# A top-k attention with two MLPs on one core: the planner's numbers set anew, two batches' value norms put at mid-run, heads and weight chunks scaled by VectorE

## The chip, the cores and the metric

The kernel runs on one core of a Trainium2 chip. The metric is the device time of one execution in microseconds (us), inputs and output in the chip's memory. The five engines are named as in the profile: PE (TensorE, with PEld for its weight loads), DVE (VectorE), ACT (ScalarE), POOL (GpSimd) and SP (SyncE, which here only issues DMAs).

## The reference

```python
scores = scale * q @ k.T                        # 4 batches, 8 heads, 576 x 64
kth = the 32nd largest of each row
attn = softmax(where(scores >= kth, scores, -1e9))
x = (attn @ v), heads side by side               # 2304 tokens x 512
h = x @ w_in                                     # 512 x 2048
g = where(h >= 1, h, where(h <= -1, 0, (h + 1)**2 / 4))
y = g @ w_out                                    # 2048 x 512
h2 = maximum(y @ w2_in, 0)
out = (h2 * h2) @ w2_out
```

All inputs and the output are float32. The result is to be close to float32, so that each operand is scaled by a power of two and split in a high and a low half in float16; a product is then three float16 matmuls.

## The kernel before

Tokens go in 18 tiles T of 128; tiles 4 and 13 hold the end of one batch and the start of the next, 64 rows each. A tile and a head make a slot, 144 in all. In a slot PE makes the scores (`s`, four matmuls, eight in tiles 4 and 13), DVE finds the 32 largest of each row with four MAX8 and three MATCH_REPLACE8, POOL makes a bias `nb`, ACT makes mask, exponential and the high half `pc`, POOL the low half, SP turns `pc` by a DMA (`pT`), and PE multiplies with the values (14 matmuls, called attend). After four heads `x_part` takes the reciprocal sums (`rs`) and scales the heads from PSUM to `x`.

The MLPs run behind, one group (a quarter of a tile's hidden layer in one of the two MLPs) to a slot, from slot 12 on: 12 matmuls of 512 columns into `h` and 12 into `o`. The first `tr` tiles of each MLP make `h` already transposed, with 48 matmuls of 128 columns; for later tiles SP turns the activations (`g<-gr`).

The weights `i1`, `o1`, `i2`, `o2` come in 16 chunks each. `w_decode` packs a chunk (POOL, ACT, DVE), `w_norm` adds its squares on PE (`gram`), `w_scale` makes the scale and `w_split` scales and splits, in the way that a letter in `w_i1` to `w_o2` says: `p` has ACT write the high half and PE form the low half (a float32 matmul and a float16 one into `lo`), which ACT copies out; `a`, `g` and `q` scale in place on ACT, POOL or DVE, then ACT writes the high half and POOL subtracts for the low one; `Q` does the same as `q`. Keys and values are scaled and split likewise by `k_prep` and `v_prep`, on POOL and ACT, or on ACT and DVE for the chunks in `dk` and `dv`. Their scales come from `norm` (ACT squares with a sum) and `kv_scale` (a short chain on DVE and PE). `meet_consts`, `mlp1_consts` and `mlp2_consts` make small per-batch constants on DVE from the value scales.

Nothing is issued as it is written. Every operation is noted with a key, its step (8 steps to a slot, `at(u, ...)`), and `Book.order` simulates five in-order engines with estimated costs and takes, on each engine, the ready operation with the lowest key. So PLAN's steps and margins set the order on each engine, and the waits follow from the data. Its `slack` delays what PE takes up after another engine, past a given time; `warm` fills planned idle time of PE with dummy matmuls (`gram<-ones`). `gshift` delays MLP groups by steps.

Of the kernel before, what the change touches and what calls it, by code (L numbers as in the profile page):

```python
# [13 lines left out]
ALU = mybir.AluOpType  # L14
# [18 lines left out]


PLAN = dict(
    slack=(260, 0.5, 0.5),
    dps={'i1': 16, 'o1': 16, 'i2': 16, 'o2': 14},
    warm=(15, 300, 0.6),
    soon={'s': 8, 'att': 8, 'a': 8, 'x': 24},
    kch=(0, 0, 0, 1), vch=(0, 0, 1), scale=(0, 1, 2, 3, 4, 5), dch=(0, 1, 3), qch=(0, 0, 3, 4), k0=(-5, -4, -2),  # L40
    ka=(0, 1), qa=(0,), d0=(-8, -6, -4, -2), l0=(-9, -6), n0=(0, 1, 0, 1, 2, 3), q01=-5, v0l=0, v0k=1, lag=1, tbufs=(1, 1), v0n=(5, 7, 9, 11), v0s=14, vn=112, vnd=6,
    vnl=18, vs=276, meet=283, mc1=287, m2c0=121, m2c1=300, v0=(21, 25, 29, 33, 37, 41, 45, 49), kv1=(254, 10, 289, 6),
    kv2=(525, 17, 553, 14), kv3=(828, 10, 862, 7), knl=69, knd=4, knll=4, ksl=34, ql=58, qs=50,
    qsch=(2, 7, 8, 9, 9, 10, 28), qp0=21, qp1=6,
    dec_i1=(8, 10, 12, 14, 16, 18, 20, 22, 24, 26, 28, 30, 32, 34, 36, 38),
    dec_o1=(43, 45, 47, 49, 51, 53, 55, 57, 59, 61, 63, 65, 67, 69, 71, 73),
    dec_i2=(76, 78, 80, 82, 84, 86, 88, 90, 92, 94, 96, 98, 100, 102, 104, 106),
    dec_o2=(109, 111, 113, 115, 117, 119, 121, 123, 126, 128, 130, 136, 138, 146), li1=4, ldl=5,
    half=((15, 150, 158), (14, 161, 168)), wn=1, ws_i1=45, ws_o1=80, ws_i2=113, ws_o2=183, sp_i1=55, sp_o1=87,
    sp_i2=120, sp_o2=190, spch=(0, 0, 1), spd_i1=8, spd_o1=8, spd_i2=8, spd_o2=8, mc0=55, N0=12, early=0,  # L50
    gshift=(0, 0, 0, 0, 0, 0, 0, 0, 0, 0, 0, 3, 3, 3, 3, 1), xu=4, xch=(0, 1, 2, 4, 4, 5),
    ych=(0, 1, 2, 3, 5, 6, 10, 10, 73), yu=36, ou=28, z0=200, g_in=(9, 9, 9, 9), g_out=(20, 22, 23, 26), g_act=11,
    g_gate=13, g_split=15, scores=-6, below=8, wbufs=4, md=(), exp=9, bias=7, phi=10, plo=11, ptr=13, att=30, acopy=29, li1d=3, lo1=0, lo1d=0, xu0=2,
    dk=(0, 1, 2), dv=(8, 11, 5, 7), dq=(), odd=0, klead=10, vlead=5, sbufs=3,
    vbufs=8,
    w_i1="pppppppppppppppp", w_o1="pgpgpgpgpgpgpgpg", w_i2="agagagagagagagag", w_o2="agagagagagagagag",
    phd=(), ghd=(), sq=(), u0=-6,
    prio=(3, 0, 0, 2, 2, 3, 4, 5, 5, 1, 7), gbufs=(2, 2), tr=(3, 3), p_tr=18, p_out=8, p_end=4,
)


# [89 lines left out]
class Book:  # L151
# [37 lines left out]
    def note(self, engine, method, fn, args, kwargs):  # L189
# [57 lines left out]
        deps.discard(op.n)  # L247
        op.deps = deps
        op.banks = {v.tile for v in views if v.tile.ring.psum}
        if engine == "POOL" or engine == "DVE" and sum(not v.tile.ring.psum for v in ins if v.elements() > 64) > 1:  # L250
            op.banks.add("port")
        if method == "dma_start_transpose":
            op.banks.add("turn")
# [36 lines left out]
    def order(self):  # L290
# [36 lines left out]
        while len(out) < len(ops):  # L327
            best = None
            for e in engines:
                if now[e]:  # L330
                    t = free[e]
                elif soon[e]:
                    t = max(free[e], soon[e][0][0])
                else:
                    continue
                if best is None or t < best[0]:
                    best = (t, e)
            if best is None:
                raise RuntimeError("no order: " + "; ".join(f"{r.kwargs['tag']}: {len(r.waiting)}" for r in self.rings.values() if r.waiting))
            t, e = best  # L340
            while soon[e] and soon[e][0][0] <= t:
                op = ops[heapq.heappop(soon[e])[1]]
                heapq.heappush(now[e], (op.key, op.n))
            op = ops[heapq.heappop(now[e])[1]]
            if not taken.isdisjoint(op.opens):
                shut.append(op)
                free[e] = t
                continue
            later = apart(op, t)
            if later > t:  # L350
# [12 lines left out]
            if op.load:
                wire = max(wire, t + 1.6) + took
                end = wire + 0.7
            elif op.move == "dma_start_transpose":
                wire = max(wire, t + 1.1) + took
                end = wire + 0.4
            else:
                end = t + took  # L370
            for b in op.banks:
                held.setdefault(b, {})[e] = end + 0.08
            out.append(op)
            for n in op.succ:
                s = ops[n]
                gap = 0.03 if s.engine == e else 0.08 if s.engine != "PE" or end < PLAN["slack"][0] else PLAN["slack"][1]
                s.ready = max(s.ready, end + gap if s.engine != "PE" or e != "PE" else t)
                s.missing -= 1
                if not s.missing:
                    ask(s)  # L380
            for r in op.tiles:
                r.left -= 1
                r.end = max(r.end, end + 0.08)
                if not r.left:
                    ring = r.ring
                    while ring.waiting and not ring.given[-ring.bufs].left:
                        ask(ops[heapq.heappop(ring.waiting)[1]])
# [32 lines left out]
def tile_topk_attention_mlp_mlp(  # L420
# [269 lines left out]
    def kv_scale(name, b):  # L690
        s, i = kvs[name]
        n2 = kvn2[name][:, b, 0:NNORM] if b == 0 else kvn2[name][:, b]
        return global_scale(s[:, b : b + 1], i[:, b : b + 1], n2, f"{name}{b}")

# [70 lines left out]
    def v_prep(b, h):  # L767
        on_dve = 8 * b + h in PLAN["dv"]

        def scale():  # L770
            t = ld["v", b, h]
            if not on_dve:
                POOL.tensor_scalar(t, t, sv[:, b : b + 1], 1.0, op0=ALU.mult, op1=ALU.mult)
            vs = pool.tile([P, 2, 5, D1], F16, tag="vst", name=f"vst_{b}_{h}", bufs=PLAN["vbufs"])
            POOL.memset(vs[:, 0, :, D : D + 1], 1.0)
            POOL.memset(vs[:, 1, :, D : D + 1], 0.0)
            vst[b, h] = vs

        def split_hi():
            ACT.activation(vst[b, h][:, 0, :, 0:D], ld["v", b, h].rearrange("p (c d) -> p c d", d=D), AF.Copy, **(dict(scale=sv[:, b : b + 1]) if on_dve else {}))  # L780

        def split_lo():
            vs = vst[b, h]
            t3 = ld.pop(("v", b, h)).rearrange("p (c d) -> p c d", d=D)
            if on_dve:
                DVE.scalar_tensor_tensor(
                    vs[:, 1, :, 0:D], t3, sv[:, b : b + 1], vs[:, 0, :, 0:D], op0=ALU.mult, op1=ALU.subtract
                )
            else:
                POOL.tensor_tensor(vs[:, 1, :, 0:D], t3, vs[:, 0, :, 0:D], op=ALU.subtract)  # L790
# [227 lines left out]
    def x_part(T, half):  # L1018
# [18 lines left out]
        def scale():  # L1037
# [3 lines left out]
            if T in (4, 13):  # L1041
                to = x[64 * half : 64 * half + 64].rearrange("p (j b a) d -> p a b j d", a=2, b=2)
                for b in range(2):
                    for a in range(2):
# [33 lines left out]

    def mlp1_consts(c0, c1):
# [244 lines left out]
        at(PLAN["v0n"][i], norm, 0, i, "v")  # L1324
    chain(PLAN["v0s"], SCALE, kv_scale, "v", 0)
    for i in range(6 * NNORM):
        at(PLAN["vn"] + PLAN["vnd"] * i - PLAN["vnl"], norm_load, v, 1 + i // (2 * NNORM), i % (2 * NNORM), "v")
        at(PLAN["vn"] + PLAN["vnd"] * i, norm, 1 + i // (2 * NNORM), i % (2 * NNORM), "v")
    for b in range(1, B):
        chain(PLAN["vs"] - 12 + 6 * (b - 1), SCALE, kv_scale, "v", b)  # L1330
    chain(PLAN["meet"], range(4), meet_consts)
    chain(PLAN["mc1"], range(11), mlp1_consts, 1, 6)
    chain(PLAN["m2c0"], range(3), mlp2_consts, 0, 1)
    chain(PLAN["m2c1"], range(3), mlp2_consts, 1, 6)
    for h in range(8):
        v_chain(0, h, PLAN["v0"][h])
    for b in (1, 2, 3):
# [153 lines left out]
```

## Time and profile before

| | us |
|---|---|
| median of three runs | 1086.64 (1085.31 to 1087.84) |
| the profiled execution | 1082.34 |
| its span, first to last instruction | 1080.5 |

The profile is of one execution, 1.84 us of which lie around the span. It counts an engine as busy while an instruction of it runs; the chain of waits goes back from the last instruction, at each step to what released it. All operations are recorded through one helper, so that every row has line 407, and the rows are told apart by tile names.

### The profile page before, as it was taken

To read this page: it belongs to the slowest core of one execution; us is meant where nothing else is said; L and a number is where in the kernel's file an instruction comes from. 1 tells how busy PE (TensorE), PEld (TensorE's weight loads), DVE (VectorE), ACT (ScalarE), POOL (GpSimd) and SP (SyncE) were. 2 spreads that over 40 slices of the span, in tenths; PEclk is the share of its full clock that TensorE was granted. 3 is DMA by queue.
4 is the path that set the end of the run, shared out by engine and by line. 5 is a ranking of instruction groups with operands and counts; after the bars stand their busy time and mean duration, and the time that the engine had idled before them with its cause. 6 is when DMAs were issued, how large, how long until landed. Compare 5 with 4: busy or idle time off the path is not lost.

```text
span 1080.5 us, 23997 instructions
## 1 busy us (share of the span) xinstructions
PE 1009.5 (93%) x8426; PEld 555.3 (51%) x8426; DVE 901.9 (83%) x1992; ACT 866.0 (80%) x1605; POOL 673.5 (62%) x1056
## 2 busy tenths in 40 slices
PE   3977789889999999999999999999999999999997
PEld 2853467666555654544444545444444444544443
DVE  4999886988899999999999999999899999991100
ACT  4679998999878788877988897988688888875442
POOL 3595878879776665657785665667674646553221
PEclk9999999999999999999999999999999999999999
DMA  8999876764667486889977677788776675664333
GB/s 222 309 339 230 234 217 161 128 145 89 137 123 136 82 135 125 169 132 165 178 138 141 117 134 135 158 150 171 135 144 135 115 134 106 125 111 90 69 66 62
DMA packets 438057, 159.14 MB, mean 147 GB/s; under 512 B 416432, under 2 KB 423600, under 8 KB 437936
## 3 DMA queue, kind: packets, MB, share of 16 engines
q1 hardware_dynamic: 434512, 156.76, 70.9%
q10 hardware_dynamic: 3424, 0.85, 0.5%
q8 instruction: 66, 1.08, 0.4%
q14 instruction: 55, 0.45, 0.1%
HBM read 55.31 MB, written 4.72 MB: 56 GB/s over the span
## 4 chain that ended last, share of the span: by engine, by line
PE 66%; ACT 9%; DMA 8%; POOL 7%; DVE 5%; issue 4%; SPq 1%; POOLq 0%; DVEq 0%; ACTq 0%
PE h L407 28%; PE o L407 27%; PE s L407 9%; DMA pT<-pc 3%; POOL wall L407 3%; ACT wall L407 2%; DVE m L407 2%; ACT W L407 2%; DVE W L407 1%; POOL pc L407 1%; PE gram_i L407 1%; ACT r L407 1%; ACT pc L407 1%; DVE wall L407 1%; PE lo_i L407 1%
## 5 line engine op out<-in xcount | busy, mean ns | idle before, releaser
L407 PE MATMUL o<-wall,g 128*128 128x512 f16 x1728 | 434.4, 380 | 7.6 <-POOL g L407 2.1
L407 DVE MAX8 m<-W 128x8 f32<-128x576 f32 x432 | 325.0, 756 | 6.7
L407 PEld LDWEIGHTS <-g 128*128 128x128 f16 x1728 | 160.7, 98 | 192.3 <-issue 11.4
L407 POOL TENSOR_TENSOR pc<-W,pc 128x64 f16<-128x64 f32 (+1 forms) x288 | 205.8, 736 | 66.7 <-ACT pc L407 62.0
L407 POOL TENSOR_TENSOR gr<-r,gr 128x512 f16<-128x512 f32 x120 | 139.3, 1161 | 163.3 <-ACT gr L407 148.8
L407 DVE MATCH_REPLACE8 W<-m,W 128x576 f32<-128x576 f32 x288 | 213.8, 743 | 0.0
L407 PE MATMUL h<-wall,T_x 128*128 128x512 f16 x720 | 168.5, 379 | 0.0
L407 PE MATMUL h<-wall,T_y 128*128 128x512 f16 x720 | 168.0, 379 | 0.0
L407 ACT ACTIVATE W<-W,nb,esc 128x576 f32<-128x576 f32 x144 | 124.4, 864 | 14.5 <-POOL nb L407 9.1
L407 ACT ACTIVATE W<-s,m 128x576 f32<-128x576 f32 x144 | 105.9, 736 | 30.0 <-DVE m L407 21.1
L407 DVE MAX8 m<-s 128x8 f32<-128x576 f32 x144 | 109.2, 759 | 22.1 <-PE s L407 17.4
L407 PEld LDWEIGHTS <-T_y 128*128 128x128 f16 x720 | 69.4, 98 | 81.1
L407 PEld LDWEIGHTS <-pT 128*128 128x128 f16 (+1 forms) x2240 | 82.7, 100 | 54.5 <-issue 15.0
L407 PEld LDWEIGHTS <-wall 128*128 128x128 f16 (+1 forms) x1408 | 85.7, 100 | 48.3 <-DVE wall L407 23.5
L407 PEld LDWEIGHTS <-T_x 128*128 128x128 f16 x720 | 69.0, 98 | 80.0 <-issue 0.4
L407 DVE MATCH_REPLACE8 W<-m,s 128x576 f32<-128x576 f32 x144 | 107.6, 748 | 0.0
L407 PE MATMUL s<-kst,qT 128*128 128x64 f16 (+3 forms) x640 | 98.2, 290 | 9.8 <-ACT W L407 7.8
L407 POOL TENSOR_SCALAR nb<-m,esc 128x1 f32<-128x1 f32 x144 | 53.4, 371 | 85.5 <-DVE m L407 67.9
L407 PE MATMUL s<-vst,pT 128*128 128x65 f16 (+1 forms) x2240 | 90.2, 194 | 15.3 <-DMA pT<-pc 8.6
L407 ACT ACTIVATE pc<-W 128x576 f16<-128x576 f32 x144 | 97.5, 677 | 1.9 <-DMA pT<-pc 0.3
L407 ACT ACTIVATE r<-r 128x512 f32<-128x512 f32 x144 | 90.5, 629 | 2.5
L407 DVE SCALAR_TENSOR_TENSOR r<-h,G,r 128x512 f32<-128x512 f32 x72 | 53.5, 743 | 46.3 <-ACT h L407 45.9
(151 smaller groups left out, 1308.4 us busy)
## 6 DMA issues: line engine op xcount, KB each, us to landing
wall<-in_moe_w_in_dram SPq DMA_DIRECT2D x32, 512.0 KB, 6.3
wall<-in_moe_w_out_dram SPq DMA_DIRECT2D x30, 512.0 KB, 5.1
out_dram<-ob SPq DMA_DIRECT2D x18, 256.0 KB, 2.5
l_q<-in_q_dram SPq DMA_DIRECT2D x16, 256.0 KB, 3.6
n_v<-in_v_dram SPq DMA_DIRECT2D x24, 144.0 KB, 3.1
n_k<-in_k_dram SPq DMA_DIRECT2D x12, 288.0 KB, 3.3
l_k<-in_k_dram SPq DMA_DIRECT2D x12, 288.0 KB, 3.4
pT<-pc SPq DMA_TRANSPOSE x144, 3.3
```

What stands on the lines that cost most here:

```text
L407: op.fn(*(real(a) for a in op.args), **{k: real(a) for k, a in op.kwargs.items()})
```

## The change

These values of PLAN change, among others (letters and steps as above):

| key | before | after |
|---|---|---|
| `vn, vnd` (norms of values, batches 1 to 3) | 112, 6: 24 in a row | 180, 9 for batch 1; `vn2, vnd2` 341, 7 for 2 and 3 |
| `vs`, `meet`, `mc1`, `m2c1` (value scales, constants) | 276, 283, 287, 300 for batches 1 to 3 | 264, 273, 277, 296 for batch 1; `vs2, meet2, mc2, m2c2` 478, 495, 500, 513 for 2 and 3 |
| `xd` (tiles whose heads DVE scales) | only 4 and 13, always | 1, 2, 3, 4, 7, 12, 13, 15, 16 |
| `w_i1` | `p` x16 | `ppgpgpgppppppgpg` |
| `w_o1` | `pgpgpgpgpgpgpgpg` | `pgpgpqpgpgpgpgpg` |
| `w_i2` | `agagagagagagagag` | `agagagagqgagagag` |
| `w_o2` | `agagagagagagagag` | `agagaqqQqgqgqqqg` |
| `dk`, `dv` (chunks split on DVE) | 0 to 2; 5, 7, 8, 11 | 4, 6, 15 added; 12, 27 added |
| `ka`, `qa` (first turns of k, q issued by ACT) | (0, 1), (0) | none: all by SP |
| `tr` | (3, 3) | (4, 3) |
| `gshift` of groups 11 to 15 | 3, 3, 3, 3, 1 | 5, 8, 7, 9, 5 |
| `gshift` of groups 16 to 34 | 0 | 4, but 0 for 20 and 2 for 34 |
| `slack` | (260, 0.5, 0.5) | (230, 0.5, 1.0) |
| `pad` (added to the planned landing of loads, of turns) | | (0, 0.7) |
| `dps` of i1 (chunks decoded by way of PSUM) | 16 | 14 |
| steps of the decodes `dec_i1` to `dec_o2`, of `v0`, `kv1` to `kv3`, `prio`, `p_end` | | each moved a little |

The code that goes with it:

```diff
+            elif T in PLAN["xd"]:
+                to = x.rearrange("p (j a) d -> p a j d", a=2)[:, :, 2 * half : 2 * half + 2]
+                for b in range(2):
+                    DVE.tensor_tensor(
+                        to[:, b], ACC[b][:, i0 : i0 + 2, 0:D], pairs[:, b].unsqueeze(2).to_broadcast([P, 2, D]), op=ALU.mult
+                    )
             else:
                 for j in sorted(js, key=lambda j: j % 2):
                     ACT.activation(x[:, j], ACC[j % 2][:, i0 + j // 2 % 2, 0:D], AF.Copy, scale=rs[:, j : j + 1])
...
             elif op.move == "dma_start_transpose":
                 wire = max(wire, t + 1.1) + took
-                end = wire + 0.4
+                end = wire + 0.4 + PLAN["pad"][1] + (PLAN["late"][1] if wire > PLAN["late"][0] else 0.0)
...
-    for b in range(1, B):
-        chain(PLAN["vs"] - 12 + 6 * (b - 1), SCALE, kv_scale, "v", b)
-    chain(PLAN["meet"], range(4), meet_consts)
-    chain(PLAN["mc1"], range(11), mlp1_consts, 1, 6)
+        late = i >= 2 * NNORM
+        u = PLAN["vn2"] + PLAN["vnd2"] * (i - 2 * NNORM) if late else PLAN["vn"] + PLAN["vnd"] * i
+        at(u - PLAN["vnl"], norm_load, v, 1 + i // (2 * NNORM), i % (2 * NNORM), "v")
+        at(u, norm, 1 + i // (2 * NNORM), i % (2 * NNORM), "v")
+    chain(PLAN["vs"], SCALE, kv_scale, "v", 1)
+    for b in (2, 3):
+        chain(PLAN["vs2"] + 6 * (b - 2), SCALE, kv_scale, "v", b)
+    chain(PLAN["meet"], range(4), meet_consts, 0)
+    chain(PLAN["meet2"], range(4), meet_consts, 1)
+    chain(PLAN["mc1"], range(11), mlp1_consts, 1, 3)
+    chain(PLAN["mc2"], range(11), mlp1_consts, 3, 6)
     chain(PLAN["m2c0"], range(3), mlp2_consts, 0, 1)
-    chain(PLAN["m2c1"], range(3), mlp2_consts, 1, 6)
+    chain(PLAN["m2c1"], range(3), mlp2_consts, 1, 3)
+    chain(PLAN["m2c2"], range(3), mlp2_consts, 3, 6)
```

The columns of the value scales and constants are put in another order (`vcol`), so that batches 0 and 1 with their shared tile lie in columns 0 to 2 and batches 2 and 3 with theirs in 3 to 5. `w_diag` gets a tile of its own for weights without a place in `DIAG_AT`. The key `late` adds 0.0.

## Rows read from the trace of the kernel before

**Rows 1.** The page: span, and busy time of each engine.
```profile
span 1080.5 us, 23997 instructions
...
PE 1009.5 (93%) x8426; PEld 555.3 (51%) x8426; DVE 901.9 (83%) x1992; ACT 866.0 (80%) x1605; POOL 673.5 (62%) x1056
```
**Rows 2.** Windows: length, busy PE, PEld, DVE, ACT, POOL, clock, DMA share, GB/s.
```profile
60.00:140.00 80.00, 61.87 (x607) 37.80 (x606) 73.38 (x171) 73.58 (x140) 60.08 (x95) 0.98 0.94 261
140.00:274.00 134.00, 115.74 (x1488) 86.63 (x1486) 111.51 (x251) 126.90 (x266) 113.85 (x151) 0.96 0.65 144
...
274.00:352.00 78.00, 75.81 (x831) 44.43 (x829) 75.47 (x188) 63.36 (x116) 55.90 (x100) 1.00 0.71 134
300.00:320.00 20.00, 18.21 (x208) 10.41 (x206) 19.60 (x57) 14.03 (x26) 14.91 (x32) 1.00 0.77 142
352.00:950.00 598.00, 592.77 (x4283) 294.88 (x4281) 568.08 (x1221) 501.60 (x909) 375.18 (x596) 1.00 0.75 137
950.00:1081.00 131.00, 125.00 (x667) 57.95 (x665) 30.32 (x67) 65.69 (x111) 38.28 (x48) 1.00 0.41 79
```
**Rows 3.** Chain of waits by line, of 140 to 274 and of 352 to 950.
```profile
by line: POOL wall L407 17.5%; DMA pT<-pc 7.5%; ACT wall L407 7.4%; issue 7.0%; POOL pc L407 6.1%; POOL g L407 5.4%; DMA wall<-in_moe_w_out_dram 3.9%; PE h L407 3.2%; DVE m L407 3.2%; ACT W L407 2.8%; DMA n_v<-in_v_dram 2.7%; ACT r L407 2.6
...
by line: PE h L407 37.1%; PE o L407 36.6%; PE s L407 13.6%; issue 2.2%; ACT r L407 1.1%; ACT W L407 1.1%; DMA l_v<-in_v_dram 0.8%; DMA kst<-khl 0.8%; DMA T_x<-hl_x 0.8%; POOL gr L407 0.8%; DMA n_k<-in_k_dram 0.5%; DMA g<-gr 0.5%; POOL pc L4
```
**Rows 4.** Chain of waits of the whole span, in order of time: start, duration, what.
```profile
274.35 2.75 PE o L407 x12
...
285.53 2.68 PE h L407 x48
...
1001.49 2.59 PE h L407 x12
```
**Rows 5.** Timeline, first 37 us: start, duration, engine, operation, idle time before.
```profile
11.86 1.34 ACTq L407 DMA_TRANSPOSE qT<-qhl  x1
...
13.26 0.77 ACT L407 ACTIVATE wall<-wall,sk 128x576 f16<-128x576 f32 x1 [1.42 <-issue]
...
22.81 1.41 SPq L407 DMA_TRANSPOSE kst<-wall  x1
...
23.09 0.77 DVE L407 MAX8 m<-s 128x8 f32<-128x576 f32 x1 [2.09 <-PE s L407]
```
**Rows 6.** Waits of SP's queue, first 27 us: total, times, longest.
```profile
SPq L407 <- DMA kst<-wall: 15.7, 1, 15.7
```
**Rows 7.** ACT's groups by form, whole span: busy, mean ns, idle before.
```profile
L407 ACT ACTIVATE x<-s,rs 128x64 f32<-128x64 f32 x128 | 32.3, 314 | 6.9 <-DVE rs L407 3.6 <-DVE sq L407 1.1 <-PE h L407 0.9
...
L407 ACT ACTIVATE wall<-lo_i 128x512 f16<-128x512 f32 x16 | 9.3, 590 | 0.1
...
L407 ACT ACTIVATE wall<-wall,s_o 128x512 f32<-128x512 f32 x8 | 5.6, 714 | 0.0
```
**Rows 8.** Windows of tile n_v alone: length, busy DVE, ACT, clock, DMA.
```profile
140.00:274.00 134.00, 0.28 (x2) 10.98 (x43) 0.96 0.65 144
```
**Rows 9.** DVE's groups by form, whole span.
```profile
L407 DVE SCALAR_TENSOR_TENSOR wall<-dec_i,wall 128x512 int32<-128x512 int32 x32 | 21.4, 680 | 7.2 <-ACT dec_i L407 5.8 <-POOL vst L407 0.6 <-POOL nb L407 0.5
...
L407 DVE TENSOR_TENSOR x<-s,rs 64x128 f32<-64x128 f32 x16 | 4.6, 286 | 0.3
L407 DVE SCALAR_TENSOR_TENSOR wall<-wall,sk 128x576 f16<-128x576 f32 x3 | 2.8, 976 | 0.0
```
**Rows 10.** Timeline of DVE, 306 to 316.
```profile
306.92 0.14 DVE L407 TENSOR_TENSOR sv<-sv 128x2 f32<-128x2 f32 x1
...
313.29 1.15 DVE L407 TENSOR_SCALAR AZ<-AZ,is_o 128x5 f32<-128x5 f32 x1
...
315.03 0.20 DVE L407 TENSOR_SCALAR AZ<-AZ,is_i 128x5 f32<-128x5 f32 x1
```
**Rows 11.** POOL's groups by form, whole span.
```profile
L407 POOL TENSOR_TENSOR wall<-wall 128x512 f16<-128x512 f32 x40 | 46.6, 1164 | 1.9 <-ACT wall L407 1.9
...
L407 POOL TENSOR_SCALAR wall<-wall,s_o 128x512 f32<-128x512 f32 x16 | 11.0, 695 | 0.7 <-DVE s_o L407 0.3
```

More of the change, by code (lines that the diff above doesn't have):

```diff
@@ L35 @@
 PLAN = dict(
[L36 to L58, printed above, removed]
+    slack=(230, 0.5, 1.0), late=(260, 0.0), dps={'i1': 14, 'o1': 16, 'i2': 16, 'o2': 14}, pad=(0, 0.7), xd=(1, 2, 3, 4, 7, 12, 13, 15, 16), warm=(15,
+    300, 0.6), port=-8, soon={'s': 8, 'att': 10, 'a': 8, 'x': 24, 'out': 0, 'dec': 0, 'n': 2}, kch=(0, 0, 0, 1), vch=(0, 0, 1), scale=(0, 1, 2, 3, 4,
@@ new lines @@
+    5), dch=(0, 1, 3), qch=(0, 0, 3, 4), k0=(-5, -4, -2), ka=(), qa=(), d0=(-8, -6, -4, -2), l0=(-9, -6), n0=(0, 1, 0, 1, 2, 3), q01=-5, v0l=-1,
+    v0k=1, lag=1, tbufs=(1, 1), v0n=(5, 7, 9, 11), v0s=15, vn=180, vnd=9, vnl=18, vs=264, vn2=341, vnd2=7, vs2=478, meet2=495, mc2=500, m2c2=513,
+    meet=273, mc1=277, m2c0=121, m2c1=296, v0=(21, 25, 29, 33, 33, 37, 41, 41), kv1=(251, 10, 288, 6), kv2=(531, 17, 553, 14), kv3=(828, 10, 859, 7),
+    knl=74, knd=4, knll=4, ksl=33, ql=58, qs=50, qsch=(2, 7, 8, 9, 9, 10, 28), qp0=21, qp1=6, dec_i1=(11, 13, 15, 17, 19, 21, 23, 25, 25, 30, 32, 34,
@@ new lines @@
+    31, 34, 35, 38), dec_o1=(49, 51, 52, 54, 55, 57, 59, 60, 62, 63, 65, 67, 68, 70, 71, 73), dec_i2=(79, 81, 83, 85, 86, 88, 90, 92, 93, 95, 97, 99,
+    101, 102, 104, 106), dec_o2=(105, 107, 109, 112, 114, 116, 119, 120, 124, 126, 128, 135, 137, 146), li1=4, ldl=4, half=((15, 150, 158), (14, 161,
+    169)), wn=1, ws_i1=47, ws_o1=80, ws_i2=114, ws_o2=183, sp_i1=55, sp_o1=87, sp_i2=120, sp_o2=190, spch=(0, 0, 1), spd_i1=8, spd_o1=8, spd_i2=8,
+    spd_o2=8, mc0=55, N0=12, early=0, gshift=(0, 0, 0, 0, 0, 0, 0, 0, 0, 0, 0, 5, 8, 7, 9, 5, 4, 4, 4, 4, 0, 4, 4, 4, 4, 4, 4, 4, 4, 4, 4, 4, 4, 4, 2,
@@ new lines @@
+    0, 0, 0, 0, 0, 0, 0, 0, 0, 1, 0, 0, -1, 0, 0, 0, 0, 0, 0, 0, 0, 0, 0, 0, 0, 0, 0, 0, 0, 0, 0, 0, 0, 0, 0, 0, 4, 4, 7, 4, 4, 0, 0, 0, 0, 0, 0, 4,
+    0, 0, 0, 0, 0, 1, 0, 0), xu=4, xch=(0, 1, 2, 4, 5, 6), ych=(0, 1, 2, 3, 5, 6, 10, 10, 73), yu=36, ou=28, z0=200, g_in=(9, 9, 9, 9), g_out=(20, 22,
+    23, 26), g_act=11, g_gate=13, g_split=15, scores=-6, below=8, wbufs=4, md=(), exp=9, bias=7, phi=10, plo=11, ptr=13, att=30, acopy=29, li1d=3,
+    lo1=0, lo1d=2, xu0=0, dk=(0, 1, 2, 4, 6, 15), dv=(5, 7, 8, 11, 12, 27), dq=(), odd=0, klead=10, vlead=6, sbufs=3, vbufs=8,
@@ L59 @@
+    w_i1='ppgpgpgppppppgpg', w_o1='pgpgpqpgpgpgpgpg', w_i2='agagagagqgagagag', w_o2='agagaqqQqgqgqqqg', phd=(), ghd=(), sq=(), u0=-6, prio=(5, 0, 0,
+    2, 2, 6, 1, 3, 5, 1, 7), gbufs=(2, 2), tr=(4, 3), p_tr=18, p_out=8, p_end=3,
 )
@@ L249, in note @@
         op.banks = {v.tile for v in views if v.tile.ring.psum}
-        if engine == "POOL" or engine == "DVE" and sum(not v.tile.ring.psum for v in ins if v.elements() > 64) > 1:
+        if engine == "POOL" or self.step >= PLAN["port"] and engine == "DVE" and sum(not v.tile.ring.psum for v in ins if v.elements() > 64) > 1:
             op.banks.add("port")
@@ L364, in order @@
                 wire = max(wire, t + 1.6) + took
-                end = wire + 0.7
+                end = wire + 0.7 + PLAN["pad"][0]
             elif op.move == "dma_start_transpose":
                 wire = max(wire, t + 1.1) + took
-                end = wire + 0.4
+                end = wire + 0.4 + PLAN["pad"][1] + (PLAN["late"][1] if wire > PLAN["late"][0] else 0.0)
             else:
@@ L596, in w_diag @@
     def w_diag(name, half):
-        at = DIAG_AT[name][half]
+        at = DIAG_AT[name][half] if name in DIAG_AT else None
         if (name, at) not in diags:
-            diags[name, at] = wall[:, at, 0:P]
+            diags[name, at] = ctile(f"diag_{name}", P) if at is None else wall[:, at, 0:P]
             DVE.tensor_scalar(diags[name, at], ident, W[name]["s"], None, op0=ALU.mult)
@@ L667, in tile_topk_attention_mlp_mlp @@
     kvs = {"k": (sk, isk), "v": (sv, isv)}
+    vcol = (0, 1, 3, 4)
     kvn2 = {n: ctile(f"n2_{n}", B * m).rearrange("p (b i) -> p b i", b=B) for n, m in (("k", NNORM), ("v", 2 * NNORM))}
@@ L692, in kv_scale @@
         n2 = kvn2[name][:, b, 0:NNORM] if b == 0 else kvn2[name][:, b]
-        return global_scale(s[:, b : b + 1], i[:, b : b + 1], n2, f"{name}{b}")
+        c = vcol[b] if name == "v" else b
+        return global_scale(s[:, c : c + 1], i[:, c : c + 1], n2, f"{name}{b}")
     def k_load(b, i):
@@ L772, in scale @@
             if not on_dve:
-                POOL.tensor_scalar(t, t, sv[:, b : b + 1], 1.0, op0=ALU.mult, op1=ALU.mult)
+                POOL.tensor_scalar(t, t, sv[:, vcol[b] : vcol[b] + 1], 1.0, op0=ALU.mult, op1=ALU.mult)
             vs = pool.tile([P, 2, 5, D1], F16, tag="vst", name=f"vst_{b}_{h}", bufs=PLAN["vbufs"])
@@ L779, in split_hi @@
         def split_hi():
-            ACT.activation(vst[b, h][:, 0, :, 0:D], ld["v", b, h].rearrange("p (c d) -> p c d", d=D), AF.Copy, **(dict(scale=sv[:, b : b + 1]) if on_dve else {}))
+            ACT.activation(vst[b, h][:, 0, :, 0:D], ld["v", b, h].rearrange("p (c d) -> p c d", d=D), AF.Copy, **(dict(scale=sv[:, vcol[b] : vcol[b] + 1]) if on_dve else {}))
         def split_lo():
@@ L786, in split_lo @@
                 DVE.scalar_tensor_tensor(
-                    vs[:, 1, :, 0:D], t3, sv[:, b : b + 1], vs[:, 0, :, 0:D], op0=ALU.mult, op1=ALU.subtract
+                    vs[:, 1, :, 0:D], t3, sv[:, vcol[b] : vcol[b] + 1], vs[:, 0, :, 0:D], op0=ALU.mult, op1=ALU.subtract
                 )
@@ L1066, in column, with meet_consts @@
     def column(T):
-        return slice(4, 5) if T == 4 else slice(5, 6) if T == 13 else slice(tile_parts(T, 0)[0][2], tile_parts(T, 0)[0][2] + 1)
-    def meet_consts():
-        ev, od, two = slice(0, B, 2), slice(1, B, 2), slice(B, 6)
+        c = 2 if T == 4 else 5 if T == 13 else vcol[tile_parts(T, 0)[0][2]]
+        return slice(c, c + 1)
+    def meet_consts(p):
+        ev, od, two = (slice(3 * p + i, 3 * p + i + 1) for i in range(3))
         tt = DVE.tensor_tensor
@@ L1074, in meet_consts @@
             lambda: tt(isv[:, two], isv[:, ev], isv[:, od], op=ALU.max),
-            lambda: tt(meets[:, ev], sv[:, two], isv[:, ev], op=ALU.mult),
-            lambda: tt(meets[:, od], sv[:, two], isv[:, od], op=ALU.mult),
+            lambda: tt(meets[:, 2 * p : 2 * p + 1], sv[:, two], isv[:, ev], op=ALU.mult),
+            lambda: tt(meets[:, 2 * p + 1 : 2 * p + 2], sv[:, two], isv[:, od], op=ALU.mult),
         ]
@@ L1326, in tile_topk_attention_mlp_mlp @@
     for i in range(6 * NNORM):
-        at(PLAN["vn"] + PLAN["vnd"] * i - PLAN["vnl"], norm_load, v, 1 + i // (2 * NNORM), i % (2 * NNORM), "v")
-        at(PLAN["vn"] + PLAN["vnd"] * i, norm, 1 + i // (2 * NNORM), i % (2 * NNORM), "v")
-    for b in range(1, B):
-        chain(PLAN["vs"] - 12 + 6 * (b - 1), SCALE, kv_scale, "v", b)
-    chain(PLAN["meet"], range(4), meet_consts)
-    chain(PLAN["mc1"], range(11), mlp1_consts, 1, 6)
+        late = i >= 2 * NNORM
[9 more added lines that the diff above has]
+    chain(PLAN["mc2"], range(11), mlp1_consts, 3, 6)
     chain(PLAN["m2c0"], range(3), mlp2_consts, 0, 1)
-    chain(PLAN["m2c1"], range(3), mlp2_consts, 1, 6)
+    chain(PLAN["m2c1"], range(3), mlp2_consts, 1, 3)
+    chain(PLAN["m2c2"], range(3), mlp2_consts, 3, 6)
     for h in range(8):
```

## The prediction

> **What bounds the kernel now.** I read the page first: PE is busy 1009.5 us of a span of 1080.5 us, but DVE (901.9) and ACT (866.0) are not far behind [rows 1], so an average over the span does not say which of them sets the time. The windows do. From 352 to 950 us PE is busy 592.8 of 598 us; from 140 to 274 us it is busy only 115.7 of 134, and there ACT has 126.9 (95%), POOL 113.9 (85%) and DVE 111.5 (83%) [rows 2]. So there are two regimes, and the chain of waits shows where they meet: in time order it goes through the MLP's matmuls from 274.35 us on [rows 4], and for 352 to 950 us PE's lines for `h`, `o` and `s` make 87% of it, while for 140 to 274 us it goes from POOL (29% in its three named lines) to DMA to ACT and back [rows 3]. The matmuls run at the full clock there: 12 of 512 columns take 2.59 us, 216 ns each [rows 4].
>
> The reader is to see this: after 274 us nothing but PE's own work counts, and 806 us of span lie behind that point. A change can gain by reaching that point sooner, by taking away the little that PE still idles behind it (5.2 us from 352 to 950, 6.0 in the tail after 950 [rows 2]), or not at all. It loses whatever it makes PE idle there, for PE has nothing to catch up with.
>
> **The change part by part.**
>
> *Start.* ACT's queue issues three turns by itself, 1.34 us for the first, and the scaling of the first keys (13.26 us) begins after 1.42 us in which ACT waits for nothing else [rows 5]. SP's queue meanwhile stands 15.7 us until ACT's turns have landed [rows 6], and issues its own first one at 22.81 us; the first MAX8 is at 23.09 after 2.09 us of idle DVE [rows 5]. With all turns on SP, ACT's 1.42 us are gone for certain, and SP can issue a turn as soon as its halves are there. The gain lies between 0 (DVE's decodes come first anyway) and 4.0 us (three issues of 1.34). I take 2.0: nearest to the 1.42 and 2.09 that the rows show idle. DVE is 92% busy behind it (60 to 140 us [rows 2]), so a start that comes sooner is kept.
>
> *60 to 140 us.* Five chunks of `i1` go from `p` to `g`. Each saves ACT a copy of 0.59 us [rows 7] and PE two matmuls, and gives POOL a scaling and a subtraction, 0.70 + 1.16 us [rows 11]. ACT falls from 73.6 to 70.6 us and POOL rises by 9.3 to 69.4 of 80, under the others. DVE, 73.4 of 80 [rows 2], gets one scaling of `o1` more and stays the fullest. So I cost this at nothing: the relief of ACT and PE hides behind DVE, and POOL's burden in its own idle 19.9 us. If POOL's gaps lie elsewhere than its new work, up to 2 us are lost; if ACT was the one that DVE waited for, up to 2.9 are won. The decodes, `v0` and the loads of `o1` that move by a few steps, and the two chunks that are no longer decoded by way of PSUM (`dps`), issue the same instructions on the same engines; SP issues nothing more. I cost them at nothing too: they move within DVE's full queue.
>
> *140 to 274 us.* Four things leave ACT. (a) Value norms: tile `n_v` takes 10.98 us of ACT here in 43 instructions, a square and a read of the sum for each norm [rows 8], so 21.5 of the 24 norms; 8 of the 24 stay here, and 13.5 x 0.51 = 6.9 us go. (b) Heads of tiles 1 and 2 (tile 3's fall behind 274): 16 x 0.25 (32.3 us over 128 [rows 7]) = 4.0. (c) `o2`: five scalings `a` at 0.70 [rows 7] = 3.5. (d) `i2`: one, 0.7. ACT falls by 15.1 to 111.8. DVE gets eight instructions for the heads, each a pair of heads from PSUM; the nearest row is 0.29 us for the like on 64 rows [rows 9]: 2.3. It gets nine scalings of 512 columns (eight of `o2`, one of `i2`). No row shows that operation on DVE. The nearest one with 512 columns is 0.68 us [rows 9]; below, a short one is 0.14 [rows 10]; above, it first stands until a subtraction of POOL is through, 0.68 + 1.16 = 1.84. I take 0.68: 6.1. DVE rises to 119.9 of 134 and is then the fullest. POOL loses three scalings (2.1). With the fullest engine as full as ACT is now (126.9/134 = 0.947), the stretch takes 119.9/0.947 = 126.6 us, 7.4 less; as full as DVE from 274 to 352 (75.5/78 = 0.968 [rows 2]), 123.9, 10.1 less; at the other end nothing, if the handing on between POOL, DMA and ACT sets the pace and not ACT's load. I take 6.5, near the first: all three engines lie under 90% then.
>
> Of DVE's scaling the trace holds a warning: in the row of short constants one took 1.15 us where its neighbour of the same shape took 0.20 [rows 10], which is the length of one subtraction on POOL, 1.16 [rows 11]. The Trainium skill says so too (SBUF — State Buffer, "Who interferes with whom"): VectorE and GpSimd share a pair of SBUF ports as an exclusive lock, and a `tensor_scalar` in a two-port mode, or an instruction with two SBUF inputs, stands until a running GpSimd instruction is through; by that rule each of the nine would cost the upper price. That is the last of the rivals below.
>
> *MLP groups put off.* `gshift` puts groups 11 to 33 off by 4 to 9 steps, mostly 4, half a slot. Behind the point of saturation a matmul that was put off is lost: half a group is 12 matmuls, 2.6 us; nine steps are 5.8. Before it, PE has 18.3 us of idle time [rows 2] that covers it. The point falls into this run of groups, so I take half of 2.6: +1.3. Tile 3 of the first MLP with `tr` 4: four groups at 48 matmuls in 2.68 instead of 12 in 2.59 us [rows 4], +0.4, and four turns less for SP.
>
> *274 to 352 us.* DVE is 75.5 of 78 full. Two key chunks (0.98 each [rows 9]), a value chunk of 5/9 that size and half of tile 3's heads come to it, some 3 us; two value scales leave, seven short instructions each at 0.14 or more [rows 10], some 2 to 3. Between 0 and +1.0; I take +0.5.
>
> *Mid-run.* The constants are made twice. The 18 instructions from 306.92 to 315.03 us took 5.5 us of DVE together, the longest 1.15 [rows 10]; in the window around them PE was idle 1.8 of 20 us, against 5.2 in all 598 later on [rows 2]. The first set stays; the second falls on a saturated PE, with DVE 95% busy there (568.1 of 598 [rows 2]). Queued behind it on DVE are the MAX8 of two slots, and PE's next scores behind those. I take the same again, +1.8, between 0 and 3.6. The 16 norms moved here cost ACT 8 us where it is 84% busy (501.6 of 598 [rows 2]): nothing, and if that cover were gone, at most the wait of one mask. The heads of tiles 7, 12, 15 and 16 and the chunks of batch 3 bring DVE some 6 us, hidden in the 30 that it idles from 352 to 950.
>
> *Margins.* `pad` and `slack` only reorder PE: what hangs on a turn or on another engine comes later in its queue. They can take away at most the 5.2 us of idle PE from 352 to 950 and some of the 2.2 from 274 to 352 [rows 2]; at worst nothing. I take 2.5. The tail, 6.0 us of idle PE after 950, I leave: its last turn and store stay.
>
> Sum: -2.0 + 0 - 6.5 + 1.3 + 0.4 + 0.5 + 1.8 - 2.5 = -7.0 us. On the profiled execution: span 1080.5 to 1073.5, time 1082.34 to 1075.3. The median of the runs stands 4.3 us above that execution, so 1086.64 - 7.0 = **1079.6**.
>
> **The rivals.** *More than forecast*: PE's idle 18.3 us were stalls of the same kind as ACT's queue, and the stretch gets as full as DVE is later (-10.1), the start gives 3.5, the margins 4.5, nothing is lost with groups put off: -15.4 with the other terms, some 1071. For it: no engine is above 90% then. Against: ACT's relief ends at DVE's 119.9.
> *Relief that is hidden anyway*: from 140 to 274 us the chain spends 29% in POOL's lines and 14% in DMA, ACT's named ones only 13% [rows 3]; ACT may be full because others make it wait and then bunch. The stretch gains nothing: -0.5, 1086.1, no change.
> *Slower, DVE and POOL in each other's way*: the nine scalings fall where POOL subtracts the same weights. At 1.84 each they are 16.6 us, DVE has 130.4, and at 0.947 the stretch takes 137.7, 3.7 more in place of 6.5 less: +3.2, 1089.8. It decides from where DVE has ACT's old 126.9: (126.9 - 111.5 - 2.3)/9 = 1.46 us each. For it speaks the 1.15 us instruction [rows 10]; against it that most of the 18 took 0.14 to 0.22, with POOL no idler (14.9 of 20 [rows 2]).
>
> **How the numbers follow.** Forecast 0.46 (1075 to 1084, its own range), more than forecast 0.22, hidden 0.16, slower 0.16. The bounds: all good ends give -4.0 - 2.9 - 10.1 - 7.4 + 0.4 = -24; all bad ends +2 + 3.7 + 5.8 + 0.4 + 1 + 3.6 = +16.5; neither is likely whole. 1067 to 1090 leaves some 2 in 10 out. About 0.2%, 2.2 us, is what a measurement of this kernel tells from no change: faster 0.68, same 0.16, slower 0.16.
>
> **What the profile of the changed kernel would show.** Right: the chain turns to PE alone before 270 us; ACT under 90% from 140 us to there with DVE the fullest; scalings of 512 columns on DVE at about 0.7 us; first MAX8 at about 21 us; a gap of a microsecond or two in PE near the second set of constants; from 352 us on less than 5 us of idle PE. Wrong: slot 32's first MAX8 no sooner than 274 us; DVE's scalings above 1.46 us; PE idle in several places behind the point where it fills.

## The result, and the profile after

| | before | after |
|---|---|---|
| median, four runs each | 1085.97 us | 1068.32 us |
| range | 1082.61 to 1087.84 | 1067.43 to 1069.53 |
| profiled execution | 1082.34 | 1068.74 |

The ratio is 0.9842, 95% interval [0.9815, 0.9869]: 17 us faster, where 7 were forecast. The sign and the range held; the size did not. The profiled execution of the kernel before was one of its shorter ones, so that the two traces differ by 13.5 us of span and not by 17.

The page of the changed kernel, span and busy times; they answer to [rows 1]:

```profile
span 1067.0 us, 24296 instructions
...
PE 1000.5 (94%) x8576; PEld 560.1 (52%) x8576; DVE 915.3 (86%) x2053; ACT 847.4 (79%) x1538; POOL 673.1 (63%) x1052
```

DVE does 13.4 us more in all, ACT 18.6 less. The same stretches as in [rows 2] (columns: length, PE, PEld, DVE, ACT, POOL, clock, DMA share, GB/s):

```profile
60.00:140.00 80.00, 62.82 (x717) 43.96 (x716) 74.89 (x174) 68.80 (x126) 66.10 (x99) 0.94 0.96 239
140.00:274.00 134.00, 121.87 (x1557) 88.28 (x1558) 128.08 (x290) 123.99 (x234) 119.72 (x155) 1.00 0.66 144
274.00:352.00 78.00, 70.65 (x938) 49.05 (x936) 76.55 (x184) 60.49 (x113) 50.74 (x96) 1.00 0.69 119
...
352.00:950.00 598.00, 595.57 (x4245) 294.50 (x4242) 571.89 (x1268) 499.36 (x901) 370.93 (x594) 1.00 0.77 140
```

From 140 to 274 us DVE is now busy 128.1 us, 96%, where it had 111.5. ACT is still at 124.0: it has less to do for each slot, but more slots pass. Between 274 and 352 us PE idles 7.4 us, more than the 2.2 of [rows 2]; from 352 to 950 it idles 2.4 in place of 5.2.

Windows of equal time hold unequal work, so I also cut both traces at the same slots: from the first MAX8 of slot 0 to that of slot 44. First the kernel before, then the changed one, same columns:

```profile
23.10:351.50 328.40, 286.11 (x3445) 198.87 (x3443) 294.14 (x683) 284.90 (x559) 249.38 (x385) 0.98 0.78 187
```

```profile
20.70:341.50 320.80, 275.96 (x3587) 201.62 (x3585) 305.34 (x699) 269.57 (x498) 254.03 (x383) 0.98 0.78 182
```

This is the place of most of the gain. DVE does 11.2 us more for the same 44 slots, and they take 7.6 us less: its idle time fell from 34.3 to 15.5 us. With 2.4 us from the start, 2.6 between slots 44 and 143 and 0.9 after the last slot this makes the 13.5.

The first MAX8 of slot 20 divides the stretch once more (before, then changed):

```profile
186.92 0.77 DVE L407 MAX8 m<-s 128x8 f32<-128x576 f32 x1 [1.18 <-PE s L407]
```

```profile
175.99 0.75 DVE L400 MAX8 m<-s 128x8 f32<-128x576 f32 x1
```

From slot 0 to slot 20 the changed kernel takes 155.3 us for 163.8, and from slot 20 to slot 44 165.5 for 164.6. What is gained up to slot 44 is there by slot 20.

Two things differ between the traces besides. One wait of DVE is all but gone, that of the MLP's `r` for ACT's part of it, `h`; in DVE's queue the top-k of later slots stands behind it. From 60 to 290 us (total, times, longest), before and then changed:

```profile
DVE r L407 <- ACT h L407: 9.1, 3, 3.5
```

```profile
DVE r L400 <- ACT h L400: 0.4, 1, 0.4
```

And PE does 9.0 us less in all (1000.5 for 1009.5), while its idle time falls by only 4.5 (66.5 for 71.0). Most of the work that went is that of the five chunks of `i1` whose low half PE no longer makes. Tile `lo_i` from 60 to 140 us (length, PE, PEld, ACT, clock, DMA share, GB/s), before and then changed:

```profile
60.00:140.00 80.00, 21.91 (x48) 4.92 (x32) 9.34 (x16) 0.98 0.94 261
```

```profile
60.00:140.00 80.00, 15.62 (x33) 3.37 (x22) 6.47 (x11) 0.94 0.96 239
```

The start and the first MAX8 of slot 32, in the timeline of the changed kernel (start, duration, engine, operation, idle time before); they answer to [rows 5] and to the 274.21 us of that MAX8 before:

```profile
11.18 1.35 SPq L400 DMA_TRANSPOSE qT<-qhl  x1
...
11.62 0.76 ACT L400 ACTIVATE wall<-wall,sk 128x576 f16<-128x576 f32 x1
...
13.26 8.49 SPq L400 DMA_TRANSPOSE kst<-wall  x4
...
20.68 1.58 DVE L400 MAX8 m<-s 128x8 f32<-128x576 f32 x2 [0.77 <-PE s L400]
...
258.97 0.76 DVE L400 MAX8 m<-s 128x8 f32<-128x576 f32 x1
```

The operations that the trace of before did not have, or had at another size, in DVE's groups by form (busy, mean ns, idle before):

```profile
L400 DVE TENSOR_TENSOR x<-s,rs 128x128 f32<-128x128 f32 x28 | 7.4, 281 | 0.0
L400 DVE TENSOR_SCALAR wall<-wall,s_o 128x512 f32<-128x512 f32 x9 | 6.8, 756 | 0.0
...
L400 DVE TENSOR_SCALAR AZ<-AZ,is_o 128x2 f32<-128x2 f32 x1 | 1.2, 1174 | 0.0
```

### The profile page after: what moved, and what is told of

Same layout as the page of the kernel before. It is cut to its first block, busy times and chain, and to the rows that moved or that the text cites. A ratio compares the mean times of both kernels' runs of the same rounds, so it can differ in the third digit from the quotient of the medians.

```text
span 1067.0 us, 24296 instructions
## 1 busy us (share of the span) xinstructions
PE 1000.5 (94%) x8576; PEld 560.1 (52%) x8576; DVE 915.3 (86%) x2053; ACT 847.4 (79%) x1538; POOL 673.1 (63%) x1052
## 4 chain that ended last, share of the span: by engine, by line
PE 66%; ACT 9%; DVE 7%; DMA 6%; POOL 6%; issue 4%; SPq 1%; POOLq 0%; ACTq 0%; DVEq 0%
PE h L400 28%; PE o L400 28%; PE s L400 9%; DVE m L400 2%; DVE W L400 2%; ACT wall L400 2%; ACT W L400 2%; POOL wall L400 2%; DMA l_q<-in_q_dram 2%; POOL pc L400 1%; DMA pT<-pc 1%; SPq L400 1%; ACT r L400 1%; DMA wall<-in_moe_w_in_dram 1%; DMA l_v<-in_v_dram 1%
## 5 line engine op out<-in xcount | busy, mean ns | idle before, releaser
L400 POOL TENSOR_TENSOR gr<-r,gr 128x512 f16<-128x512 f32 x116 | 134.3, 1158 | 155.8 <-ACT gr L400 138.2
L400 PE MATMUL h<-wall,T_x 128*128 128x512 f16 x672 | 156.3, 379 | 0.0
L400 PEld LDWEIGHTS <-wall 128*128 128x128 f16 (+1 forms) x1600 | 96.5, 98 | 43.2 <-DVE wall L400 11.1
L400 PE MATMUL s<-kst,qT 128*128 128x64 f16 (+3 forms) x640 | 96.0, 290 | 16.5 <-ACT W L400 16.0
L400 PEld LDWEIGHTS <-T_x 128*128 128x128 f16 x672 | 65.0, 98 | 76.8
L400 PE MATMUL s<-vst,pT 128*128 128x65 f16 (+1 forms) x2240 | 92.4, 194 | 10.1 <-DMA pT<-pc 5.3
L400 ACT ACTIVATE r<-h,B,A 128x512 f32<-128x512 f32 x72 | 55.8, 774 | 38.0 <-PE h L400 38.0
```

The costliest lines, as they stand in the source:

```text
L400: op.fn(*(real(a) for a in op.args), **{k: real(a) for k, a in op.kwargs.items()})
```

## The experiments

Each run was timed against the kernel before on the same chip; the changed kernel stands at 0.9842 of it. Where I give microseconds for a ratio or a difference of two, they are of 1087 us.

**One engine made lighter, every order kept.** The planner still saw the full operations, so each queue has its old order; only the instructions issued are shorter or, on PE, left out.

```diff
 square_norm(t, kvn2[name][:, b, i : i + 1], junk)             # e_light_act; and the scalings `a` of i2, o2
+if b and name == "v": book.ops[-1].args = (junk[:, 0:16], t[:, 0:16], ...)
...
-ops.append(lambda src=src, mi=mi: DVE.max(mi, src))           # e_light_dve, i == 1, slots 16 to 31
+DVE.max(mi, src); book.ops[-1].args = (mi, src[:, 0:64])
...
 POOL.tensor_scalar(src, src, s, 1.0, ...)                     # e_light_pool, i2 and o2
+book.ops[-1].args = (src[:, 0:16], src[:, 0:16], ...)
...
 PE.matmul(ps[1], ps[0], src, start=True, stop=False)          # e_light_pe
+book.ops[-1].fn = lambda *args, **kwargs: None
 PE.matmul(ps[1], neg, hi, start=False, stop=True)
+book.ops[-1].kwargs = dict(start=True, stop=True)
```

> The kernel before with every engine's order as it was, but ACT's work in the ACT-full stretch made shorter: the 24 value norms square 16 of 288 columns, the 16 scalings on ACT of i2 and o2 touch 16 of 512 columns (part of the computation is left out). That takes about 12 us of ACT out of 140 to 274 us and gives no engine anything. Load theory (ACT's load set the pace there): 6 to 10 us faster than before, slot 32 some 6 to 10 us sooner. Order theory (the gain came from the steps and margins, that is from who stands behind whom in the queues): under 3 us faster.

> The kernel before with every engine's order as it was, but the second MAX8 of slots 16 to 31 reads 64 of 576 columns (part of the computation is left out): about 8 us less of DVE in the stretch in which 8.6 us less of ACT moved no slot. Theory that DVE's top-k is the pacer there (its queue stands behind waiting instructions and loses the time for good): slot 32 some 5 to 8 us sooner, 4 to 8 us faster. Theory that no engine's load matters there but only who waits for whom: under 2 us.

> The kernel before with every engine's order as it was, but POOL's 16 scalings of i2 and o2 touch 16 of 512 columns (part of the computation is left out): about 9 us less of POOL, whose lines led the chain of waits from 140 to 274 us. If the chain of POOL's lines sets the pace there: 4 us or more faster. If DVE is the pacer: under 2 us.

> The kernel before with every engine's order as it was, but the float32 matmul of the 24 p chunks left out (the low halves are then wrong): some 30 us less of PE between 60 and 150 us. If PE's time for the p chunks is on the path there: 4 us or more faster. If, as with ACT, DVE and POOL, no single engine's load sets the pace under a fixed order: under 2 us.

| engine made lighter | ratio | 95% interval |
|---|---|---|
| ACT | 0.9980 | [0.9963, 0.9996] |
| DVE | 0.9985 | [0.9965, 1.0006] |
| POOL | 0.9981 | [0.9964, 0.9999] |
| PE | 1.0018 | [1.0005, 1.0030] |

Windows of the first three, 140 to 274 us, in this order (columns as above):

```profile
140.00:274.00 134.00, 116.26 (x1490) 86.49 (x1489) 112.95 (x252) 118.31 (x265) 114.07 (x152) 0.96 0.65 144
```

```profile
140.00:274.00 134.00, 115.25 (x1482) 86.48 (x1481) 105.22 (x252) 126.42 (x262) 112.84 (x151) 0.96 0.65 145
```

```profile
140.00:274.00 134.00, 116.00 (x1469) 86.24 (x1468) 111.65 (x251) 124.93 (x261) 106.19 (x150) 0.95 0.67 144
```

Against [rows 2] ACT lost 8.6 us, DVE 6.3 and POOL 7.7, and the time that was freed became idle time. Slot 32 begins no sooner than at 274.21 us. Its first MAX8, in the timelines of the runs with the lighter ACT, DVE and POOL:

```profile
274.31 0.76 DVE L407 MAX8 m<-s 128x8 f32<-128x576 f32 x1
```

```profile
275.93 0.76 DVE L407 MAX8 m<-s 128x8 f32<-128x576 f32 x1
```

```profile
276.99 0.76 DVE L407 MAX8 m<-s 128x8 f32<-128x576 f32 x1
```

DVE's wait for `h` is 9.5 us with the lighter ACT, as long as before. So the load theory falls for ACT, and the rival theory that DVE's load is the pacer falls with it: with the orders fixed and one engine made lighter at a time, some 2 us of the 6 to 9 come through, at most 4 by the intervals, for whichever of the three. PE's run does not settle PE: its clock fell with its work (last section).

**Work and steps apart.** `e_moves_only` has the work moved and before's steps and margins; `e_steps_only` the reverse, with one set of constants.

```diff
+PLAN.update(gshift=(0, ... 3, 3, 3, 3, 1), slack=(260, 0.5, 0.5), pad=(0, 0.0), prio=..., dec_i1=..., kv1=..., ...)    # e_moves_only
+PLAN.update(vn=112, vnd=6, vn2=160, vs=264, ..., xd=(), w_i1="p" * 16, ..., ka=(0, 1), qa=(0,), tr=(3, 3))             # e_steps_only
```

> The changed kernel with the work moved as in the change (norms, heads, weight chunks, key and value chunks, turns on SP, tr, dps), but with the steps and margins of before (gshift, slack, pad, soon, prio, decode and key steps, p_end and the like). Load theory: at least 12 of the 17.6 us remain, some 1070 to 1074. Order theory: under 6 us faster than before, 1080 or more.

> The changed kernel's steps and margins, but the work where it was before (value norms early and one set of constants, heads on ACT, weight letters, chunks, turns and tr of before). Load theory: at most 5 us faster than before, 1081 or more. Order theory: 11 us or more faster, 1075 or less.

Measured 0.9943 [0.9925, 0.9962] and 0.9962 [0.9947, 0.9977]: 6 and 4 us, 10 together, where the whole change has 17. The moves alone fall far short of the 12 us of the load theory, and the steps alone of the 11 of the order theory, so neither holds by itself. It looks as if the two halves need each other. These two runs alone do not show it: each is a new order of all instructions, and a new order by itself was worth up to 4 us (below).

**One part undone in the changed kernel.**

```diff
+PLAN.update(vn=112, vnd=6, vn2=160, vnd2=6, vs2=270, meet=283, ...)     # e_no_norms, one set of constants
+PLAN.update(gshift=(0, 0, 0, 0, 0, 0, 0, 0, 0, 0, 0, 3, 3, 3, 3, 1))    # e_no_gshift
+PLAN.update(w_i1="pppppppppppppppp", w_o1="pgpg...", ...)               # e_no_letters
+PLAN.update(w_i1="pppppppppppppppp")                                    # e_no_i1
+PLAN.update(slack=(260, 0.5, 0.5), pad=(0, 0.0))                        # e_no_margins
```

> The changed kernel with only the value norms of all three batches back at their early steps and one set of constants, as before: 6.9 us of ACT return to 140 to 274 us, the second set of constants goes. Load theory: 4 to 7 us slower than the changed kernel, 1072 to 1075. Order theory: within 2 us of it, or faster by the second set of constants.

> The changed kernel with gshift as before. Prediction on record priced the new gshift as a loss of 1.3 us: then this is 1 to 2 us faster than the changed kernel. If the later groups keep DVE's gate instructions from standing ahead of the top-k while they wait: 3 us or more slower, with more idle DVE between slots 16 and 36.

> The changed kernel with the letters of all four weights as before: ACT gets 7 us back, DVE loses 10 scalings (7.5 us), POOL the five chunks of i1. If ACT's relief was what helped: 3 to 6 us slower. If DVE's own load is what counts: no slower, up to 5 us faster, since DVE does less.

> The changed kernel with only the letters of i1 as before (16 times p). The prediction on record costed the five chunks at nothing. If so: within 2 us of the changed kernel, and the 8.6 us that all letters cost lie in o1, i2 and o2. If the way of a p chunk (ACT, PE's float32 matmul in order, ACT again, with one of two h buffers held) is what holds up the start of the MLP: 5 us or more slower, and slot 16 some 4 to 6 us later.

> The changed kernel with slack (260, 0.5, 0.5) and no added planned landing for turns, as before. The prediction on record: 2.5 us slower than the changed kernel, from idle PE behind 352 us. If the margins also keep early instructions from standing ahead of others: 5 us or more slower.

| undone | ratio | 95% interval | against 0.9842 |
|---|---|---|---|
| value norms, second constants | 0.9851 | [0.9823, 0.9880] | +1.0 us, intervals overlap |
| `gshift` | 0.9822 | [0.9804, 0.9840] | -2.2 us, intervals overlap |
| all weight letters | 0.9892 | [0.9868, 0.9916] | +5.4 us, intervals just touch |
| letters of `i1` | 0.9939 | [0.9916, 0.9962] | +10.5 us |
| margins | 0.9962 | [0.9940, 0.9984] | +13.0 us |

Two parts that I costed at nothing and at 2.5 us are the dear ones. (`e_no_gshift` also drops the shifts of some groups behind 34, which the table of the change leaves out.)

Without the letters of `i1` slot 12 begins 1.2 us later than in the changed kernel, slot 16 begins 6.3 us and slot 20 7.6 us later. So much of their price is there by the time that the MLPs have started. Slot 16, changed and then without the letters:

```profile
143.18 0.75 DVE L400 MAX8 m<-s 128x8 f32<-128x576 f32 x1
```

```profile
149.45 0.76 DVE L403 MAX8 m<-s 128x8 f32<-128x576 f32 x1
```

One thing that the margins change is PE's wait for turns from 60 to 274 us (total, times, longest), first the changed kernel, then the one without its margins:

```profile
PE s L400 <- DMA pT<-pc: 4.8, 4, 2.4
```

```profile
PE s L404 <- DMA pT<-pc: 11.7, 13, 2.8
```

PE's queue takes an attend up too soon 13 times in place of 4 and stands until the turn has landed, with whatever comes next in its queue behind it. That this makes the price is not shown. `e_after_vn` (below) waits 8.9 us in 9 and keeps the whole gain, and `e_steps_only` waits 0.2 in one and has 4 us of it. DVE's longest wait for scores without the margins, 5.5 us before slot 16, is not behind a turn either: PE was busy 5.3 us of it.

Later on PE waits for something else. Without margins it is busy 590.1 us from 352 to 950, with them 595.6; it waits 0.2 us for turns there, but 5.7 for ACT's masks (`W`), a wait that the changed kernel does not show:

```profile
PE s L404 <- ACT W L404: 5.7, 7, 2.0
```

```profile
352.00:950.00 598.00, 590.12 (x4238) 293.17 (x4237) 567.71 (x1256) 493.81 (x899) 367.71 (x587) 1.00 0.78 140
```

**Neighbouring orders.** Any edit makes the planner order all 24,000 instructions anew, so a part's price could be the luck of a draw. Four runs move one step by one and change no work.

```diff
-vn=112, vnd=6                    # e_before_vn
+vn=113, vnd=6
-dec_i1=(8, ..., 26, 28, 30, ...  # e_before_dec
+dec_i1=(8, ..., 26, 29, 30, ...
+PLAN.update(vn=181)              # e_after_vn
+PLAN.update(dec_i1=(11, ..., 30, 33, 34, ...))    # e_after_dec, 33 for 32
```

> The kernel before with the first value norm one step later (vn 113 for 112): no work is changed, only the planner's order. If an order is as good as its neighbours: within 2 us of before. If each order is a draw: 3 us or more away, on either side.

> The kernel before with one decode of i1 (chunk 10) one step later, no work changed. If an order is as good as its neighbours: within 2 us of before. If each order is a draw: 3 us or more away, on either side.

> The changed kernel with the first of the moved value norms one step later (vn 181 for 180), no work changed. If the 10 to 13 us that undoing the letters of i1 or the margins cost belong to those parts: within 2 us of the changed kernel. If the changed kernel is one good draw of the planner and any new order loses it: 5 us or more slower.

> The changed kernel with one decode of i1 (chunk 10) one step later, no work changed. As for the run before: within 2 us if the parts carry the gain, 5 us or more slower if any new order loses it.

Measured 1.0038 [1.0016, 1.0060] and 0.9970 [0.9953, 0.9988] for the neighbours of before, 0.9839 [0.9803, 0.9876] and 0.9841 [0.9805, 0.9877] for those of the changed kernel. A draw was worth up to 4 us in the kernel before, by two neighbours only. The prices of 10 and 13 us are more than that; those of the norms, of `gshift` and of all letters are not clear of it. The neighbours of the changed kernel keep its gain whole: it is no single lucky order.

**The two parts added to the kernel before.**

```diff
-w_i1="pppppppppppppppp"          # e_only_i1 and e_i1_margins
+w_i1="ppgpgpgppppppgpg"
-slack=(260, 0.5, 0.5)            # e_only_margins and e_i1_margins
+slack=(230, 0.5, 1.0)
-end = wire + 0.4
+end = wire + 0.4 + 0.7
```

> The kernel before with only the five chunks of i1 changed from p to g. If the way of a p chunk held it up by itself: 4 us or more faster than before. If it matters only with the rest of the change: within 2 us of before.

> The kernel before with only the margins of the change: slack (230, 0.5, 1.0) and 0.7 us added to the planned landing of a turn. Taken out of the changed kernel they cost 13 us. If they work by themselves: 5 us or more faster than before. If they pay only with the rest: within the 4 us by which neighbouring orders of this kernel differ.

> The kernel before with both the margins and the five chunks of i1 from p to g. If these two parts are the core of the gain: 10 us or more faster than before, of the 17.6. If the gain needs the other moves too: no more than the 4.8 us of the letters of i1 alone plus what the margins give alone.

Measured 0.9956 [0.9932, 0.9981], 0.9947 [0.9928, 0.9967] and 0.9922 [0.9892, 0.9952]: 4.8, 5.8 and 8.5 us. Each alone is little more than the 4 us of a draw; both together are twice that, and half of the gain. The other half comes only with the rest.

No kernel was found that beats the changed one beyond the intervals; `e_no_gshift` comes nearest.

## Why the prediction was off, point by point

*By place.* The forecast of 7.0 is 2.0 at the start, 4.3 from there to 352 us and 0.7 behind it. The traces have 2.4 at the start, 7.6 from there to slot 44 (351.5 us before) and 3.5 behind it. The other 4 us between the medians lie in no trace.

*What bounds the kernel.* Held: PE alone after the point of saturation, with its little idle time; 10.0 of the 13.5 us lie ahead of it.

*Start.* Forecast 2.0, measured 2.4 at the first MAX8. The scaling of the keys begins at 11.62 for 13.26, and SP issues four turns in a row from 13.26 on.

*60 to 140 us: the step that failed first.* I costed the five chunks of `i1` at nothing, because DVE was the fullest engine and stayed it. They are worth 4.8 us alone, little more than a draw, and 10.5 in the changed kernel. A `p` chunk passes ACT, PE and ACT again, each in the order of a queue; a `g` chunk passes POOL, ACT, POOL. I counted busy time and not the number of queues in which something else stands behind it. That the hand-overs make the price is argued, not shown. PE's own time is a rival that stands: it does 6.3 us less for `lo_i` in this stretch, and `e_light_pe`, which was to test it, lost its clock.

*140 to 274 us: the step that failed in its reason.* "With the fullest engine as full as ACT is now" takes ACT's 95% for the pace. It was not. 8.6 us of ACT taken away under the same order brought slot 32 no sooner and gave some 2 us in all. The Trainium skill (Perfetto Trace Analysis, "Identifying the Most-Contended Engine") has the engine with the highest occupancy optimized first; in this stretch the measurement says otherwise, with a ratio of 0.9980 for the lighter ACT. The result that DVE becomes the fullest came true, at 96%. The size of 6.5 cannot be held against one pair of slots: slots 16 to 32 take 115.8 us for 134.3, but the changed kernel begins slot 16 3.3 us later, and from slot 20 to slot 44 it gains nothing. My own rival, that ACT is full because others make it wait, fits the lighter runs better, but drew the wrong end from it: if the hand-over is the pace, then moves and margins that shorten it can be worth more than the load that they carry, not nothing.

*The norms* take 6.9 us off ACT by my count and are worth 1.0 with the second constants, not told from nothing. *The heads* cost DVE 0.28 each as forecast (0.29); what they bring was not tried alone.

*DVE's scalings, and the rival of the shared port.* Forecast 0.68 us, measured 0.76 for `o2` and `o1`, far from the 1.46 at which the rival begins. A whole subtraction of POOL ahead of each, 1.84, is not what the trace shows as the usual case, though a constant again took 1.17 us. POOL is longer beside them: three of its instructions of 512 columns that began while such a scaling ran took 1.34 to 1.35 us, where 1.16 is usual. The Trainium skill (SBUF — State Buffer, "Who interferes with whom") has whichever of DVE and POOL issues first hold their shared ports for its whole instruction, when DVE is in a two-port mode. The trace agrees in so far as one is longer beside the other, here by 0.2 us and not by a whole instruction.

*Groups put off.* Forecast +1.3. PE does idle 5 us more between 274 and 352, and yet `gshift` undone gains only 2.2 us, not told from nothing. The sign may be right.

*The second constants.* Forecast +1.8, far too much. In the window of the changed kernel around them DVE has no idle time left, and PE loses 0.1 us of 30:

```profile
450.00:480.00 30.00, 29.89 (x207) 14.90 (x206) 29.93 (x88) 21.89 (x36) 12.94 (x18) 1.00 0.68 130
```

*Margins: the term that was mis-sized most.* Forecast 2.5, from idle PE behind 274 us; worth 5.8 alone and 13 in the changed kernel. Behind 352 us PE's idle time fell by 2.8, as forecast, but without the margins it would be 5.5 us more than it is. I took margins for a matter of the saturated part. They act ahead of it too: without them slot 20 begins at 183.28 us for 175.99. That an attend taken up too soon holds back the scores and with them DVE is argued, not shown.

*What stays open.* Why the parts bring 17 us together when halves bring 10: that one late queue hides what another would give fits all runs, but no run shows which hand-over it is. DVE's wait for `h` is a candidate: it is 5.1 us or more in the kernel before and its two neighbours, and 0.6 or less in the changed kernel and its two. It is not the whole, for without margins it is 0.5, and that kernel has 4 us of the 17. The heads, the letters of `i2` and `o2` alone and the steps of the decodes were not separated. That all four letters undone cost less than those of `i1` alone suggests that letters and steps are fitted to each other; the 5 us between them are also near what a draw is worth.

## What to carry to other kernels

A high busy share of an in-order engine that several others feed is no proof that it sets the pace: make its instructions shorter under the same order, and see whether anything moves. Where nothing moves for any engine, suspect the hand-overs between queues, and look for instructions that are queued before their input is there; a fraction of a microsecond of margin in the planner was worth more here than 7 us of work taken off the fullest engine. And before a part of a plan is given a price, move one step by one, to learn how much a new order is worth by itself.

## What had not been expected of the hardware

With the float32 matmuls left out, PE was busy 52.9 us from 60 to 140 us, for 61.9 before, and its granted clock in that stretch fell from 0.98 to 0.77, so that it stood at the lower of its two levels (1.2 for 2.4 GHz) for nearly half of it, 2 x (1 - 0.77) = 0.46. In the window of `e_light_pe`:

```profile
60.00:140.00 80.00, 52.86 (x557) 36.07 (x555) 73.41 (x170) 73.38 (x140) 59.56 (x95) 0.77 0.93 259
```

The run was 0.2% slower than before, with less to do.
